# Seven block products for eight in part of a fused retention and two-FFN kernel, with weight steps over pairs of tiles

## The chip, the cores and the metric

One core of a Trainium2 chip runs the whole program. The metric is device time in microseconds, and less is better. A difference of more than 0.3% can be told from no change.

## What is computed

Block retention gives `x` (1536 tokens by 512), and two feed-forward layers follow. Only the first layer's `h` is computed in another way by the change.

```python
h = x @ w_in                                  # 1536x512 @ 512x2048
sp = np.where(h > 20.0, h, np.log1p(np.exp(np.minimum(h, 20.0))))
x = (h * np.tanh(sp)) @ w_out                 # mish; 2048x512
h = x @ w_in                                  # second layer, its own weights
return np.where(h > 0.0, h, np.exp(np.minimum(h, 0.0)) - 1.0) @ w_out
```

The weights are 64-bit floats in memory.

## The kernel before, in words

Every large matrix product is made of 128x512 matmuls on fp32r operands. Each operand is kept as two parts, a high part that ScalarE rounds (Copy to fp32r) and a low part that VectorE subtracts, and one product of two tiles is three matmuls: high by high, high by low, low by high.

After the retention (some 52 us) come two layers. A layer has 4 groups `g` of 4 tiles `i` of d_ff (128 columns each), and the tokens are 3 blocks `t` of 512. A unit is either ("in", s, i), 12 matmuls that make `h` of one tile and one token block (`mm_in`), followed by the activation and the split of `g` into two parts (`split_g`), or ("out", s, d), 12 matmuls over the group's 4 tiles (`mm_out`) whose result `flush` copies or adds to `acc`. The first group makes all 12 "in" units, then "out" of block 0 as one unit of 48 (`all_out`). After that the list `seq` alternates four "in" units of one block with four "out" units of the block before.

The weights come as 64-bit words. `w_load` brings one 128x512 tile (512 KB) into `raw`, which has 4 buffers. `w_steps` makes fp32 of it in eight VectorE instructions and one ScalarE copy, and leaves `w` with its two parts. There are 64 tiles, n = 0 to 63: per layer and group four of `w_in` (side 0) and four of `w_out` (side 1). The tables `FIRST`, `SECOND` and `LATER` say behind which unit each tile's steps are issued. A scheduler then sets the final order on each engine, and each engine runs its own list in order. The names that the engines' lists show, such as `w_1471`, are buffers: the digits tell them apart.

Of the kernel before, what the change touches and what calls it, by code (L numbers as in the profile page):

```python
# [18 lines left out]
def kernel(  # L19
# [37 lines left out]
    order = []  # L57
# [5 lines left out]
    AHEAD = 4  # L63
    wts = {}
    raw = {}

    def w_load(n, part=0, parts=1):
        if n >= NW:
            return
        l, g, side, i = order[n]  # L70
        m = g * G + i
        if part == 0:
            raw[n] = cv.tile([P, KD, P, 2], I32, tag="raw", name="raw", bufs=AHEAD)
        r = raw[n]
# [11 lines left out]
    def w_steps(n, parts=1):  # L86
        if n >= NW:
            return
        l, g, side, i = order[n]
        r = raw[n].rearrange("p k f t -> p (k f) t")  # L90
        tiles = [cv.tile([P, DM], I32, tag=x, name=x) for x in ("m", "b", "u")]
        w = wp.tile([P, 2, DM], F32R, tag=f"w{side}", name=f"w{side}", bufs=(6, 8)[side])
        for y in range(parts):
            cols = slice(y * DM // parts, (y + 1) * DM // parts)
            lw, hw = r[:, cols, 0].bitcast(U32), r[:, cols, 1]
            m, b, u = (x[:, cols] for x in tiles)
            mf, bf, uf = (x.bitcast(F32) for x in (m, b, u))
            yield nc.vector.tensor_scalar(
                out=m, in0=hw, scalar1=1, scalar2=1,
                op0=ALU.logical_shift_left, op1=ALU.logical_shift_right,  # L100
            )
            yield nc.vector.tensor_scalar(out=mf, in0=mf, scalar1=LEAST, scalar2=None, op0=ALU.max)

            yield nc.vector.tensor_scalar(  # L104
                out=b, in0=m, scalar1=3, scalar2=0x3FFFFFF8,
                op0=ALU.logical_shift_left, op1=ALU.bitwise_and,
            )
# [3 lines left out]
            yield nc.vector.tensor_scalar(  # L111
                out=u, in0=b, scalar1=-0x800000, scalar2=None, op0=ALU.bitwise_and
            )

            yield nc.vector.scalar_tensor_tensor(  # L115
                out=uf, in0=lw, scalar=2.0 ** -52, in1=uf, op0=ALU.mult, op1=ALU.mult
            )
            if n >= PG - AHEAD:
                w_load(n + AHEAD)
            yield nc.vector.tensor_tensor(out=mf, in0=bf, in1=uf, op=ALU.add)  # L120
            nc.scalar.activation(out=w[:, 0, cols], in_=mf, func=AF.Copy)  # L121
            yield nc.vector.tensor_tensor(  # L122
                out=w[:, 1, cols], in0=mf, in1=w[:, 0, cols].bitcast(F32), op=ALU.subtract
            )
        del raw[n]
        wts[l, side, g * G + i] = w


    def retention(beside_load, beside_step, at_end):
# [282 lines left out]
    gt, mid, late, acc, entered = {}, {}, {}, [], [0]  # L412

    def open_late():
        def pool(name, **kw):
            return ctx.enter_context(tc.tile_pool(name=name, reuse_waits="tile", **kw))

        late["y"] = pool("yp", bufs=1)
        late["g"] = pool("gp", bufs=12)
        late["psH"] = pool("psL", bufs=3, space=PSUM)  # L420
        late["psY"] = pool("psY", bufs=4, space=PSUM)
        acc.extend(late["y"].tile([P, KD, TB], F32, name=f"acc{t}") for t in range(NTB))

    def mm_in(s, i):
        l, g, t = steps[s]
        w = wts[l, 0, g * G + i]
        h = (late["psH"] if entered[0] % 4 else psH).tile([P, TB], F32, tag="h", name="h")
        entered[0] += 1
        for kk in range(KD):
            wa, wb = (w[:, n, kk * P:(kk + 1) * P] for n in range(2))  # L430
            xa, xb = xh[t][:, kk], xl[t][:, kk]
            for n, (lt, rt) in enumerate(((wa, xa), (wa, xb), (wb, xa))):
                nc.tensor.matmul(  # L433
                    h, lhsT=lt, rhs=rt,
                    start=(kk == 0 and n == 0), stop=(kk == KD - 1 and n == 2),
                )
        return h

    def split_g(s, i):
        g = mid.pop((s, i))  # L440
        gg = late["g"].tile([P, 2, TB], F32R, tag="g", name="g")
        nc.scalar.activation(out=gg[:, 0], in_=g, func=AF.Copy)  # L442
        nc.vector.tensor_tensor(  # L443
            out=gg[:, 1], in0=g, in1=gg[:, 0].bitcast(F32), op=ALU.subtract
        )
        gt[s, i] = gg


    def mish(s, i, h):
        g = tp.tile([P, TB], F32, tag="g32", name="g32", bufs=6)  # L450
        nc.scalar.activation(out=g, in_=h, func=AF.Mish)  # L451
        mid[s, i] = g


    def elu(s, i, h):
        e = tp.tile([P, TB], F32, tag="e", name="e", bufs=3)
        nc.scalar.activation(out=e, in_=h, func=AF.Relu, scale=-1.0)  # L457
        nc.scalar.activation(out=e, in_=e, func=AF.Exp, scale=-1.0)  # L458
        g = tp.tile([P, TB], F32, tag="g32", name="g32", bufs=6)
        nc.vector.scalar_tensor_tensor(  # L460
            out=g, in0=e, scalar=-1.0, in1=h, op0=ALU.add, op1=ALU.max
        )
        mid[s, i] = g

    def mm_out(s, d, cols):
        l, g, t = steps[s]
# [50 lines left out]

    seq = [("in", t, i) for i in range(G) for t in range(NTB)]
    HEAD = len(seq)
    tail = [("out", 0), ("out", 1)]  # L520
    for s in range(NTB, NS):
        tail += [("in", s), ("out", s - 1)]
    tail.append(("out", NS - 1))
    for kind, s in tail:
        seq += [(kind, s, x) for x in range(G if kind == "in" else KD)]

    def unit(u):
        kind, s, x = seq[u]
        if kind == "in":
            (mish, elu)[steps[s][0]](s, x, mm_in(s, x))  # L530
            if late:
                split_g(s, x)
        else:

            if s == 0:
                if x == 0:
                    all_out(s)
                return
            ends = (0, 3 * TB // 4, TB) if u == len(seq) - 1 else (0, TB)
            for c0, c1 in zip(ends, ends[1:]):  # L540
                cols = slice(c0, c1)
                flush(s, x, cols, mm_out(s, x, cols))

    FIRST = (0, 0, 0, 0, 0, 1, 3, 5)
    SECOND = (7, 9, 11, 13, 16, 18, 20, 22)
    LATER = (24, 27, 30, 33, 36, 38, 40, 44)
    EARLY = 1
    BESIDE = 4  # L550
    at = {}
    for n in range(BESIDE, NW):
        g, i = divmod(n, PG)
        u = (FIRST, SECOND)[g][i] if g < 2 else LATER[i] + (g - 2) * 24
        at.setdefault(u, []).append(n)
# [7 lines left out]
    def beside():  # L563
        for n in range(BESIDE):
            yield from w_steps(n, HALVES if n == 0 else 1)
# [5 lines left out]
            pin(w_load(*m, HALVES) if isinstance(m, tuple) else w_load(m))  # L571

    made = []

    def beside_step(n, place, pin):
        for _ in range(STEPS.get((n, place), 0)):
            made.append(pin(next(todo)))

    def weights_at(u):
        for n in at.get(u, ()):  # L580
            for _ in w_steps(n):
                pass

    def first_units():
        with tc.issue_after(made[-2].ins):
# [45 lines left out]
```

## Time and profile before

| | us |
|---|---|
| median of 3 runs | 583.49 (582.27 to 583.72) |
| the profiled execution | 583.47 |
| its span, first to last instruction | 581.3 |
| TensorE busy (matmul) | 574.7 |
| VectorE busy | 433.5 |
| ScalarE busy | 232.0 |

The 2.2 us between span and time lie around the program. Busy time counts a matmul as pipelined, so the chain of waits and the start-to-start times say more than the sum.

### The profile page before, as it was taken

To read this page: it belongs to the slowest core of one execution; us is meant where nothing else is said; L and a number is where in the kernel's file an instruction comes from. 1 tells how busy PE (TensorE), PEld (TensorE's weight loads), DVE (VectorE), ACT (ScalarE), POOL (GpSimd) and SP (SyncE) were. 2 spreads that over 40 slices of the span, in tenths; PEclk is the share of its full clock that TensorE was granted. 3 is DMA by queue.
4 is the path that set the end of the run, shared out by engine and by line. 5 is a ranking of instruction groups with operands and counts; after the bars stand their busy time and mean duration, and the time that the engine had idled before them with its cause. 6 is when DMAs were issued, how large, how long until landed. Compare 5 with 4: busy or idle time off the path is not lost.

```text
span 581.3 us, 8152 instructions
## 1 busy us (share of the span) xinstructions
PE 574.7 (99%) x3234; PEld 481.5 (83%) x3234; DVE 433.5 (75%) x806; ACT 232.0 (40%) x391; POOL 18.8 (3%) x28
## 2 busy tenths in 40 slices
PE   8999999999999999999999999999999999999997
PEld 7998888888888888888888888888888888888886
DVE  7779999999399627993599957995499957944332
ACT  4655553444124214223346446545245225335220
POOL 5330000000000000000000000000000000000000
PEclk9999999999999999999999999999999999999999
DMA  9989324333023201321022221321022300000112
GB/s 181 211 199 248 110 73 146 109 109 118 28 73 118 99 2 36 110 89 57 0 73 72 74 72 37 109 83 63 1 72 73 108 37 1 1 0 1 72 55 91
DMA packets 61045, 46.66 MB, mean 80 GB/s; under 512 B 38864, under 2 KB 55504, under 8 KB 61008
## 3 DMA queue, kind: packets, MB, share of 16 engines
q1 hardware_dynamic: 60864, 46.14, 27.6%
q8 instruction: 25, 0.41, 0.3%
q14 instruction: 12, 0.10, 0.1%
q10 hardware_dynamic: 144, 0.00, 0.0%
HBM read 43.00 MB, written 3.15 MB: 79 GB/s over the span
## 4 chain that ended last, share of the span: by engine, by line
PE 96%; DMA 2%; SPq 1%; issue 0%; DVE 0%
PE h L433 45%; PE y L475 43%; PE o L293 3%; PE y L490 2%; PE sc L279 1%; SPq L157 1%; DMA vn<-in_v_dram 1%; DMA qn<-in_q_dram 1%; PE st L325 1%; PE Tp L235 1%; DVE acc L503 0%
## 5 line engine op out<-in xcount | busy, mean ns | idle before, releaser
L433 PE MATMUL h<-xh,w 128*128 128x512 f32 x768 | 240.4, 389 | 0.0
L433 PEld LDWEIGHTS h<-xh,w 128*128 128x128 f32 x768 | 144.1, 188 | 30.1 <-issue 0.2
L433 PE MATMUL h<-xl,w 128*128 128x512 f32 x384 | 149.4, 389 | 0.0
L475 PE MATMUL y<-w,g 128*128 128x512 f32 (+2 forms) x588 | 133.0, 386 | 0.0
L475 PEld LDWEIGHTS y<-w,g 128*128 128x128 f32 x588 | 109.5, 188 | 22.1
L475 PE MATMUL y<-g,w 128*128 128x512 f32 x528 | 121.6, 389 | 0.0
L475 PEld LDWEIGHTS y<-g,w 128*128 128x128 f32 x528 | 99.1, 188 | 20.6
L503 DVE TENSOR_TENSOR acc<-acc,y 128x512 f32<-128x512 f32 (+1 forms) x73 | 49.5, 678 | 58.3 <-PE y L475 58.2
L443 DVE TENSOR_TENSOR g<-g,g 128x512 fp32r<-128x512 f32 x96 | 66.1, 688 | 28.8 <-ACT g L442 26.4
L433 PEld LDWEIGHTS h<-xl,w 128*128 128x128 f32 x384 | 72.1, 188 | 14.9
L121 ACT ACTIVATE w<-m 128x512 fp32r<-128x512 f32 (+1 forms) x65 | 40.4, 622 | 103.2 <-PE h L433 55.2
L442 ACT ACTIVATE g<-g 128x512 fp32r<-128x512 f32 x96 | 60.4, 629 | 16.4 <-DVE g L460 14.8
L122 DVE TENSOR_TENSOR w<-m,w 128x512 fp32r<-128x512 f32 (+1 forms) x65 | 44.2, 679 | 24.3 <-ACT w L121 23.7
L451 ACT ACTIVATE g<-h 128x512 f32<-128x512 f32 x48 | 28.6, 596 | 69.6 <-PE h L433 69.5
L457 ACT ACTIVATE e<-h 128x512 f32<-128x512 f32 x48 | 28.6, 597 | 59.0 <-PE h L433 58.1
L460 DVE SCALAR_TENSOR_TENSOR g<-e,h 128x512 f32<-128x512 f32 x48 | 32.8, 684 | 17.0 <-ACT e L458 17.0
L115 DVE SCALAR_TENSOR_TENSOR u<-raw,u 128x512 f32<-128x512 uint32 (+1 forms) x65 | 44.1, 678 | 0.2
L120 DVE TENSOR_TENSOR m<-b,u 128x512 f32<-128x512 f32 (+1 forms) x65 | 44.1, 678 | 0.2
L108 DVE SCALAR_TENSOR_TENSOR b<-raw,b 128x512 int32<-128x512 int32 (+1 forms) x65 | 44.0, 678 | 0.1
L458 ACT ACTIVATE e<-e 128x512 f32<-128x512 f32 x48 | 30.2, 630 | 1.1
L111 DVE TENSOR_SCALAR u<-b 128x512 int32<-128x512 int32 (+1 forms) x65 | 27.2, 418 | 0.4
L104 DVE TENSOR_SCALAR b<-m 128x512 int32<-128x512 int32 (+1 forms) x65 | 27.2, 418 | 0.4
(50 smaller groups left out, 307.1 us busy)
## 6 DMA issues: line engine op xcount, KB each, us to landing
raw<-in_moe_w_out_dram SPq DMA_DIRECT2D x32, 512.0 KB, 3.3
raw<-in_moe_w_in_dram SPq DMA_DIRECT2D x31, 512.0 KB, 3.8
vn<-in_v_dram SPq DMA_DIRECT2D x12, 256.0 KB, 5.4
kn<-in_k_dram SPq DMA_DIRECT2D x11, 256.0 KB, 5.2
qn<-in_q_dram SPq DMA_DIRECT2D x11, 256.0 KB, 5.2
out_dram<-acc SPq DMA_DIRECT2D x11, 256.0 KB, 2.0
raw<-in_moe_w_in_dram SPq DMA_DIRECT2D x2, 256.0 KB, 5.5
kn<-in_k_dram SPq DMA_DIRECT2D x2, 128.0 KB, 3.3
```

Of the source, the lines that this page charges most:

```text
L108: yield nc.vector.scalar_tensor_tensor(out=b, in0=hw, scalar=-0x40000000, in1=b, op0=ALU.bitwise_and, op1=ALU.bitwise_or)
L115: yield nc.vector.scalar_tensor_tensor(out=uf, in0=lw, scalar=2.0 ** -52, in1=uf, op0=ALU.mult, op1=ALU.mult)
L120: yield nc.vector.tensor_tensor(out=mf, in0=bf, in1=uf, op=ALU.add)
L121: nc.scalar.activation(out=w[:, 0, cols], in_=mf, func=AF.Copy)
L122: yield nc.vector.tensor_tensor(out=w[:, 1, cols], in0=mf, in1=w[:, 0, cols].bitcast(F32), op=ALU.subtract)
L433: nc.tensor.matmul(h, lhsT=lt, rhs=rt, start=(kk == 0 and n == 0), stop=(kk == KD - 1 and n == 2),)
L442: nc.scalar.activation(out=gg[:, 0], in_=g, func=AF.Copy)
L443: nc.vector.tensor_tensor(out=gg[:, 1], in0=g, in1=gg[:, 0].bitcast(F32), op=ALU.subtract)
L458: nc.scalar.activation(out=e, in_=e, func=AF.Exp, scale=-1.0)
L460: nc.vector.scalar_tensor_tensor(out=g, in0=e, scalar=-1.0, in1=h, op0=ALU.add, op1=ALU.max)
L475: nc.tensor.matmul(y, lhsT=lt, rhs=rt, start=(i == 0 and n == 0), stop=(i == G - 1 and n == 2),)
L503: nc.vector.tensor_tensor(out=dst, in0=dst, in1=y, op=ALU.add)
```

## The change

The diff makes three edits.

**Block products.** For groups 1 to 3 of the first layer, and for token blocks 1 and 2, two tiles of d_ff by two halves of the 512 input rows by the two token blocks are a 2x2 by 2x2 block product. It is computed with seven block products of 6 matmuls each (`block_product`, sums as in Strassen's method in Winograd's form) where eight were. There are two such pairs, z = 0 and 1, in each group. The sums of weight blocks (`block_sums`) are made for every pair, and the sums of token blocks (`token_sums`) once. They lie in new tiles `s`, `t2`, `t3`, `t4`, and one of them in the place of a block of `xh` and `xl`. Products that belong to several results are kept by a ScalarE copy out of their PSUM bank (`keep`), and added by VectorE (`done`). Block 0 keeps its "in" units.

**Weight steps over pairs.** The eight instructions of `w_steps` now handle two tiles, 128x1024, except for tiles 0 to 3. `raw` has two buffers of a pair each, the integer steps write back into `raw`, and the two loads of a pair are issued together when the pair two ahead is done with its buffer. The pairs of `w_out` have two buffers in the first layer.

**Order of units.** All of group 0's "out" units come first. Then each group has three "in" units of block 0, the block products of z = 0, the "out" of block 0 among those of z = 1, and the "out" of blocks 1 and 2. The place of the weight steps is in `PAIRS`.

The core of the diff:

```diff
+        if n % 2 == 0 and part == 0:
+            raw[n // 2] = cv.tile([P, 2, KD, P, 2], I32, tag="raw", name="raw")
...
+        whole = cv.tile([P, 2 * DM], I32, tag="m", name="m")
         for y in range(parts):
...
+            cols = slice(lead + y * count // parts, lead + (y + 1) * count // parts)
+            lw, b, m = r[:, cols, 0].bitcast(U32), r[:, cols, 1], whole[:, cols]
...
             yield nc.vector.scalar_tensor_tensor(
-                out=b, in0=hw, scalar=-0x40000000, in1=b, op0=ALU.bitwise_and, op1=ALU.bitwise_or
+                out=b, in0=b, scalar=-0x40000000, in1=m, op0=ALU.bitwise_and, op1=ALU.bitwise_or
             )
...
+            if both and n >= PG - 4:
+                w_load(n + 4)
+                w_load(n + 5)
+            nc.scalar.activation(out=w0, in_=mf, func=AF.Copy)
+            if both and side == 0 and mixed(l, g):
+                sums[g, i // 2] = block_sums(whole.bitcast(F32))
+            yield nc.vector.tensor_tensor(out=w1, in0=mf, in1=w0.bitcast(F32), op=ALU.subtract)
...
+    def block_sums(w):
+        x = cv.tile([P, 2 * DM], F32, tag="m", name="x")
+        s1, s2, s3, s4 = (x[:, y * 2 * P:(y + 1) * 2 * P] for y in range(4))
+        a11, a12, a21, a22 = (w[:, y * 2 * P:(y + 1) * 2 * P] for y in range(4))
+        plus(s1, a21, a22)
+        minus(s3, a11, a21)
+        minus(s2, s1, a11)
+        minus(s4, a12, s2)
+        t = late["s"].tile([P, 2, 4, 2 * P], F32R, tag="s", name="s")
+        in_two([t[:, n].rearrange("p y c -> p (y c)") for n in range(2)], x)
+        return t
...
+    def block_product(g, z, x):
...
+        bank = {1: 0, 6: 0, 7: 0, 4: 0, 2: 1, 5: 2, 3: 2}[x]
+        fresh = x in (1, 2, 5)
...
+        for kk in range(2):
+            ha, la = (t[:, kk * P:(kk + 1) * P] for t in a)
+            hb, lb = (t[:, kk] for t in b)
+            for n, (lt, rt) in enumerate(((ha, hb), (ha, lb), (la, hb))):
+                nc.tensor.matmul(
+                    ps, lhsT=lt, rhs=rt, start=fresh and kk == 0 and n == 0,
+                    stop=kk == 1 and n == 2, skip_group_check=True,
+                )
...
+        def keep(y):
+            mx[z, "c", y] = tp.tile([P, TB], F32, tag="e", name="c", bufs=ES)
+            nc.scalar.activation(out=mx[z, "c", y], in_=ps, func=AF.Copy)
+
+        def done(y, s, i):
+            c = mx[z, "c", y]
+            nc.vector.tensor_tensor(out=c, in0=c, in1=ps, op=ALU.add)
+            nc.scalar.activation(out=c, in_=c, func=AF.Mish)
...
+    MIX = ((1, 2), (6, 5), (7,), (4, 3))
...
+        seq.extend(("in", s, x) for x in range(3))
+        seq.extend(("mix", (g, 0), x) for x in range(3))
+        seq.append(("in", s, 3))
+        seq.append(("mix", (g, 0), 3))
+        seq.extend(("out", s, d) for d in range(3))
+        seq.extend(("mix", (g, 1), x) for x in range(3))
+        seq.append(("out", s, 3))
+        seq.append(("mix", (g, 1), 3))
...
+    PAIRS = {
+        0: (None, None, 0, 3), 1: (12, 12, 23, 25), 2: (37, 41, 47, 49), 3: (61, 65, 71, 73),
+        4: (82, 84, 88, 91),
+    }
+    TOKENS = 11
```

`in_two` is a ScalarE Copy to fp32r for the high part and a VectorE subtraction for the low part. `token_sums` is ten additions or subtractions of 128x1024 and four `in_two` of 128x1024.

**Where TensorE takes up the outputs of group 1.** Before, the first `w_out` tile of group 1 is `w_1471`, and its first matmuls stand behind the "in" units of two token blocks and behind the outputs of block 2 of group 0:

```order
L433 MATMUL h<-xh_65,w_1442 128x512 x2
L433 MATMUL h<-xl_68,w_1442 128x512
L433 MATMUL h<-xh_65,w_1442 128x512
L475 MATMUL y<-g,w_1471 128x512 x3
L475 MATMUL y<-g,w_1514 128x512 x3
L475 MATMUL y<-g,w_1561 128x512 x3
L475 MATMUL y<-g,w_1612 128x512 x3
```

In the change the first pair of `w_out` tiles of group 1 is `w_1530`. Its matmuls stand among the block products of z = 0 (`mby`) and z = 1 (`mbh`), whose operands are the token sums `t` and the weight sums `s`:

```order
L574 MATMUL mbh<-xh_65,w_1396 128x512
L574 MATMUL mby<-t_1297,s 128x512 x6
L574 MATMUL mby<-t_1298,s 128x512 x6
L615 MATMUL y<-g,w_1530 128x512 x4
L574 MATMUL mby<-t_1299,w_1374 128x512 x6
L574 MATMUL mbh<-xh_66,s 128x512
L574 MATMUL mbh<-xl_69,s 128x512
L574 MATMUL mbh<-xh_66,s 128x512 x2
L574 MATMUL mbh<-xl_69,s 128x512
L574 MATMUL mbh<-xh_66,s 128x512
L615 MATMUL y<-g,w_1530 128x512 x14
```

The outputs of block 2 of group 0 now stand ahead of all "in" units of group 1, so that the outputs of group 1 begin behind the "in" units of only one block and 42 matmuls of block products.

**VectorE ahead of that place.** Before, the low part of `w_1471` is subtracted between the splits of the first "in" units of group 1 (`g_1553` and `g_1586`):

```order
L120 TENSOR_TENSOR m<-b,u 128x512
L108 SCALAR_TENSOR_TENSOR b<-raw,b 128x512
L443 TENSOR_TENSOR g<-g_1553,g 128x512
L111 TENSOR_SCALAR u<-b 128x512
L122 TENSOR_TENSOR w_1471<-m,w_1471 128x512
L115 SCALAR_TENSOR_TENSOR u<-raw,u 128x512
L98 TENSOR_SCALAR m<-raw 128x512
L120 TENSOR_TENSOR m<-b,u 128x512
```

In the change the low part of `w_1530` stands behind the steps of a second pair that was taken up beside it, behind a split of a sum of products (`g<-c`) and behind the addition of products (`c<-c,mby`):

```order
L132 TENSOR_SCALAR m<-raw 128x1024
L129 SCALAR_TENSOR_TENSOR raw<-raw,m 128x1024
L587 TENSOR_TENSOR c<-c,mby 128x512
L136 SCALAR_TENSOR_TENSOR m<-raw,m 128x1024
L161 TENSOR_TENSOR g<-g_1607,g 128x512
L132 TENSOR_SCALAR m<-raw 128x1024
L139 TENSOR_TENSOR m<-raw,m 128x1024
L161 TENSOR_TENSOR g<-c,g 128x512
L136 SCALAR_TENSOR_TENSOR m<-raw,m 128x1024
L146 TENSOR_TENSOR w_1530<-m,w_1530 128x1024
L139 TENSOR_TENSOR m<-raw,m 128x1024
L587 TENSOR_TENSOR c<-c,mby 128x512
```

The subtraction has moved from the beginning of the group's "in" units to their end.

**VectorE at the token sums.** In the change this stands behind the last steps of group 0's weights (`w_1140`). The tile `acc_1082` is the scratch of the token sums, `raw` and `m` belong to the steps of group 1's first pair of `w_in`:

```order
L151 TENSOR_TENSOR acc_1082<-xh_66 128x1024
L151 TENSOR_TENSOR acc_1082<-xl_69 128x1024
L129 SCALAR_TENSOR_TENSOR raw<-raw,m 128x1024
L151 TENSOR_TENSOR acc_1082<-acc_1082 128x1024
L132 TENSOR_SCALAR m<-raw 128x1024
L151 TENSOR_TENSOR acc_1082<-xl_69,xl_68 128x1024
L136 SCALAR_TENSOR_TENSOR m<-raw,m 128x1024
L161 TENSOR_TENSOR t_1298<-acc_1082,t_1298 128x1024
L139 TENSOR_TENSOR m<-raw,m 128x1024
L151 TENSOR_TENSOR acc_1082<-xh_66,xh_65 128x1024
```

No such rows were there before.

**ScalarE at the same place as `w_1530`.** The rounding of its high part stands between two copies of products out of their PSUM bank:

```order
L583 ACTIVATE c<-mby 128x512
L160 ACTIVATE g<-g_1607 128x512
L588 ACTIVATE c<-c 128x512
L160 ACTIVATE g<-c 128x512
L583 ACTIVATE c<-mby 128x512
L143 ACTIVATE w_1530<-m 128x1024
L583 ACTIVATE c<-mby 128x512
L510 ACTIVATE g_1674<-h 128x512
```

Before, nothing but activations, splits and flushes stood around such a copy.

## Rows read from the trace of the kernel before

**Rows 1.** The page's head: busy time of each engine, and VectorE in 40 slices

```profile
span 581.3 us, 8152 instructions
PE 574.7 (99%) x3234; PEld 481.5 (83%) x3234; DVE 433.5 (75%) x806; ACT 232.0 (40%) x391; POOL 18.8 (3%) x28
...
DVE  7779999999399627993599957995499957944332
```

**Rows 2.** The chain that ended last, in order: start us, us, what

```profile
52.19 2.98 PE o L293 x48
55.17 32.89 PE h L433 x144
88.06 10.88 PE y L490 x48
...
103.70 8.16 PE y L475 x36
```

**Rows 3.** Windows of the span: us, busy time by engine, granted clock, DMA

```profile
0.00:52.00 52.00, 48.32 (x870) 45.19 (x870) 39.74 (x64) 28.24 (x47) 18.81 (x28) 1.00 0.97 205
8.00:16.00 8.00, 6.45 (x115) 5.79 (x117) 7.63 (x10) 3.69 (x6) 4.15 (x4) 1.00 1.15 202
52.00:131.00 79.00, 79.00 (x387) 65.41 (x384) 76.21 (x156) 36.30 (x63) 0.00 (x0) 1.00 0.38 120
131.00:229.00 98.00, 98.00 (x434) 81.16 (x433) 68.73 (x131) 30.66 (x51) 0.00 (x0) 1.00 0.20 65
229.00:327.00 98.00, 98.00 (x434) 81.16 (x433) 80.52 (x153) 38.43 (x63) 0.00 (x0) 1.00 0.23 70
```

**Rows 4.** VectorE's groups by form: busy us, mean ns, idle before

```profile
L108 DVE SCALAR_TENSOR_TENSOR b<-raw,b 128x512 int32<-128x512 int32 x63 | 43.2, 686 | 0.1
...
L98 DVE TENSOR_SCALAR m<-raw 128x512 int32<-128x512 int32 x63 | 26.6, 422 | 0.2
L102 DVE TENSOR_SCALAR m<-m 128x512 f32<-128x512 f32 x63 | 26.6, 422 | 0.1
...
L122 DVE TENSOR_TENSOR w<-m,w 128x256 fp32r<-128x256 f32 x2 | 0.8, 416 | 0.0
L102 DVE TENSOR_SCALAR m<-m 128x256 f32<-128x256 f32 x2 | 0.6, 294 | 0.1
```

**Rows 5.** VectorE in order of time: start us, us, what

```profile
52.81 1.22 DVE L286 TENSOR_TENSOR am<-sc,dm 128x1024 f32<-128x1024 f32 x1
53.94 0.28 DVE L111 TENSOR_SCALAR u<-b 128x256 int32<-128x256 int32 x1
...
55.99 0.42 DVE L98 TENSOR_SCALAR m<-raw 128x512 int32<-128x512 int32 x1
56.45 0.43 DVE L102 TENSOR_SCALAR m<-m 128x512 f32<-128x512 f32 x1
...
62.10 0.68 DVE L443 TENSOR_TENSOR g<-g,g 128x512 fp32r<-128x512 f32 x1
62.70 0.42 DVE L98 TENSOR_SCALAR m<-raw 128x512 int32<-128x512 int32 x1
63.04 0.68 DVE L108 SCALAR_TENSOR_TENSOR b<-raw,b 128x512 int32<-128x512 int32 x1
...
70.51 0.42 DVE L98 TENSOR_SCALAR m<-raw 128x512 int32<-128x512 int32 x1
...
114.82 0.69 DVE L122 TENSOR_TENSOR w<-m,w 128x512 fp32r<-128x512 f32 x1
```

**Rows 6.** ScalarE's groups by form

```profile
L241 ACT ACTIVATE T<-Tp 128x1024 f32<-128x1024 f32 x11 | 11.3, 1025 | 5.8 <-PE Tp L235 5.7
```

**Rows 7.** ScalarE in order of time

```profile
111.90 0.60 ACT L501 ACTIVATE acc<-y 128x512 f32<-128x512 f32 x1 [2.12 <-PE y L475]
```

**Rows 8.** DMA issues between 46 and 62 us, median us to landing

```profile
raw<-in_moe_w_in_dram SPq DMA_DIRECT2D x3, 512.0 KB, 6.3
raw<-in_moe_w_out_dram SPq DMA_DIRECT2D x2, 512.0 KB, 3.8
```

More of the change, by code (lines that the diff above doesn't have):

```diff
@@ L62, with mixed @@
     PG = 2 * G
-    AHEAD = 4
     wts = {}
     raw = {}
+    made_w = {}
+    sums = {}
+    late = {}
+    def mixed(l, g):
+        return l == 0 and g > 0
     def w_load(n, part=0, parts=1):
@@ L83, in w_load, with w_tile, w_steps @@
         return nc.sync.dma_start(out=r.rearrange("p k f t -> p (k f t)"), in_=src)
-    def w_steps(n, parts=1):
+    def w_tile(n):
+        l, g, side, i = order[n]
+        if n % 2 == 0:
+            if l == 0:
+                pool, tag, bufs = wp, f"w{side}", 2
+            elif side == 0:
+                pool, tag, bufs = wp, f"w{i // 2}", 2
+            else:
+                pool, tag, bufs = late["w"], "w2", 4
+            made_w[n // 2] = pool.tile([P, 2, 2, DM], F32R, tag=tag, name=tag, bufs=bufs)
+        return made_w[n // 2]
+    def w_steps(n, parts=1, both=False):
         if n >= NW:
@@ L117, in w_steps @@
             )
[L118 to L126, printed above, removed]
+            yield nc.vector.tensor_tensor(out=mf, in0=bf, in1=mf, op=ALU.add)
@@ new lines, in w_steps, with plus @@
+            if both and n >= PG - 4:
[5 more added lines that the diff above has]
+            yield nc.vector.tensor_tensor(out=w1, in0=mf, in1=w0.bitcast(F32), op=ALU.subtract)
+        for j in range(1 + both):
+            wts[l, side, g * G + i + j] = w[:, :, (n + j) % 2]
+    def plus(out, a, b, op=ALU.add):
+        nc.vector.tensor_tensor(
+            out=out.bitcast(F32), in0=a.bitcast(F32), in1=b.bitcast(F32), op=op
+        )
@@ L411 @@
     NS = len(steps)
-    gt, mid, late, acc, entered = {}, {}, {}, [], [0]
+    gt, mid, acc, entered = {}, {}, [], [0]
+    ES = 7
     def open_late():
@@ L437, in mm_in, with g_tile @@
         return h
-    def split_g(s, i):
[L440 to L445, printed above, removed]
+    def g_tile(s, i):
+        if s == 0 and i >= 2:
+            if i == 2:
+                first.append(late["t"].tile([P, 2, 2, TB], F32R, tag="t4", name="gt"))
+            return first[0][:, i - 2]
+        return late["g"].tile([P, 2, TB], F32R, tag="g", name="g")
@@ new lines, in block_product, with of @@
+    def block_product(g, z, x):
+        w = [wts[0, 0, g * G + 2 * z + j] for j in range(2)]
+        sm = sums[g, z]
+        def of(j, h):
+            return [w[j][:, n, h * 2 * P:(h + 1) * 2 * P] for n in range(2)]
+        a = {1: of(0, 0), 2: of(0, 1), 4: of(1, 1)}.get(x)
+        if a is None:
+            y = {5: 0, 6: 1, 7: 2, 3: 3}[x]
+            a = [sm[:, n, y] for n in range(2)]
+        b = mx["b"][x]
+        bank = {1: 0, 6: 0, 7: 0, 4: 0, 2: 1, 5: 2, 3: 2}[x]
+        fresh = x in (1, 2, 5)
+        if fresh:
+            pool, tag = ((late["psY"], "y"), (late["psH"], "h"))[z]
+            mx[z, bank] = pool.tile([P, TB], F32, tag=tag, name="mb" + tag)
+        ps = mx[z, bank]
+        for kk in range(2):
[5 more added lines that the diff above has]
+                    stop=kk == 1 and n == 2, skip_group_check=True,
+                )
+        s1, s2 = g * NTB + 1, g * NTB + 2
+        i1, i2 = 2 * z, 2 * z + 1
+        def keep(y):
[5 more added lines that the diff above has]
+            nc.scalar.activation(out=c, in_=c, func=AF.Mish)
+            mid[s, i] = c
+            split_g(s, i)
+        if x in (1, 6, 7):
+            keep({1: 1, 6: 2, 7: 3}[x])
+        if x == 2:
+            done(1, s1, i1)
+        elif x == 3:
+            done(2, s2, i1)
+        elif x == 4:
+            mish(s1, i2, ps)
+            split_g(s1, i2)
+        if x == 7:
+            ps = mx[z, 2]
+            done(3, s2, i2)
@@ L573 @@
     made = []
+    last_step = {}
     def beside_step(n, place, pin):
@@ L579, in weights_at @@
     def weights_at(u):
+        if u == LAST_MIX:
+            late["mix"].close()
+            late["w"] = ctx.enter_context(tc.tile_pool(name="w2p", reuse_waits="tile", bufs=1))
         for n in at.get(u, ()):
-            for _ in w_steps(n):
+            for last_step[n] in w_steps(n, both=True):
                 pass
+        if u == TOKENS:
+            with tc.issue_after(last_step[PG - 2].ins):
+                token_sums()
     def first_units():
```

116 lines of the change are left out of this document (80 added, 36 removed).

## The prediction

> **What bounds the kernel now.** I read the page's head first: TensorE is busy for 574.7 of 581.3 us [rows 1]. Busy time flatters matmuls, so I went to the chain of waits. From 55 us it is one run of TensorE's own matmuls, and 48 of them always take 10.88 us, 0.2267 us each [rows 2]. The windows confirm it: TensorE is idle for 3.7 us in the first 52 us, and for nothing in the stretches shown between 52 and 327 us [rows 3]. So a matmul removed is worth 0.2267 us, as long as its operands are there in time. What could make them late is VectorE, which runs the weight steps. It is busy for 76.2 of 79.0 us between 52 and 131 us, 96%, and for 70% and 82% of the next two stretches [rows 3]. It is nevertheless early there: the low part of `w_1471` is made at 114.8 us [rows 5], and its first matmul stands 240 matmuls behind the start of `all_out`, at 88.06 + 240 x 0.2267 = 142.5 us [rows 2]. That lead of 27 us is what the change can spend.
>
> **What it removes.** Per pair z, eight block products of 6 matmuls become seven. With two pairs in three groups that is 6 x 6 = 36 matmuls of 1152, of the same shape as those left: 36 x 0.2267 = **8.16 us**. By this alone the profiled execution's 583.47 us become 575.3 (span 573.1). Its time agrees with the median, 583.49, so no correction is needed.
>
> **What it adds to VectorE.** What counts is the time from one start to the next, which is shorter than the duration. A two-input instruction of 512 takes 0.60 us (62.10 to 62.70), a one-input one 0.34 (62.70 to 63.04), and 0.12 more when the next needs its result (55.99 to 56.45 is 0.46); a two-input one of 1024 takes 1.13 (52.81 to 53.94) [rows 5]. A one-input one of 256 is 0.128 us shorter than one of 512 [rows 4], so at 1024 I take 0.34 + 2 x 0.128 = 0.60. A two-input one of 256 is 0.27 shorter than one of 512 (416 against 686 ns) [rows 4], 0.33.
>
> A pair of tiles thus costs 4 x 0.60 + 4 x 1.13 = 6.9 us, against 2 x (4 x 0.34 + 4 x 0.60) = 7.5 for two single tiles. Over 30 pairs this gives back 18 us. The token sums cost 14 x 1.13 = 15.8 us once; the weight sums 4 x 0.33 + 1.13 = 2.45 us for each of six pairs, 14.7; the additions of products 18 x 0.60 = 10.8. In all VectorE has some 23 us more than its 433.5 [rows 1]. Averaged over the span that is nothing, but all the token sums and two of the weight sums fall into the stretch that is at 96%.
>
> **Where it ends on the path.** I followed VectorE's order from the first instruction that differs in size, the one on `raw` of tiles 4 and 5, at 70.51 us [rows 5]; up to there the work is the same. From it to the low part of `w_1530` there are 38 two-input instructions of 1024, 24 one-input ones of 1024, 14 two-input ones of 512 and 8 of 256, and 18 times one needs the result of the one just before: 42.9 + 14.4 + 8.4 + 2.6 + 2.2 = 70.5 us, so 141.0.
>
> To this come waits for ScalarE, which is not busy but runs in order behind copies that TensorE paces. A flush starts 0.04 us after its last matmul (111.86, the end of the chain's piece at 103.70, then 111.90) [rows 2, 7]. The rounding of the token sum that replaces `xh_66` stands behind the flush of block 1's third output, whose matmuls end at 88.06 + 84 x 0.2267 = 107.1. With 0.6 for the flush [rows 7] and 1.03 for a 1024 copy [rows 6] it is ready at 108.8, and VectorE would be there at 108.0: 0.8 us. The splits of group 1's first two "in" units end at 124.7 and 127.5 by the same working (matmuls end at 123.4 and 126.1), VectorE is there at 123.8 and 127.2: 0.9 and 0.3. Together 2.0, and the low part of `w_1530` is done at 141.0 + 2.0 + 0.1 = 143.1 us.
>
> TensorE wants it for its third `w_1530` matmul. Ahead of that, from the start of `all_out`, stand 48 matmuls of `all_out`, 96 of blocks 1 and 2, 48 "in" matmuls, 42 of block products and 2 of `w_1530`: 236 x 0.2267 = 53.5, so 141.6 us. TensorE waits for **1.5 us**. Behind that matmul in its order stand the block products of both pairs; nothing overtakes.
>
> The places ahead have more room. The low part of `w_1140` is done at 92.6 and wanted at 95.3. The first product with token and weight sums is wanted at 128.9, and its sums end by 114. Behind the wait VectorE gains on TensorE: a group has four pairs (29 us with the dependences), two weight sums (5), 6 additions, 12 splits and 12 flushes (18), 52 us in 276 matmuls or 62.6 us. In groups 2 and 3 the `w_out` pair must wait for its buffer until block 2's outputs are done; 46 matmuls (10.4 us) later it is wanted, and VectorE needs some 7 us from there. In layer 2 a group has 51 us of VectorE work in 65.3. These I cost at nothing; without that room each us late is a us lost.
>
> **Loads.** They are as many and as large, but two are issued at once, when a pair's buffer is done. For tiles 6 and 7 VectorE asks 5.0 us after that, for 8 and 9 5.3 us. Single loads land after 3.8 us, three issued close together after 6.3 [rows 8]. I take something between for two and no wait; by 6.3 it is 1.3 + 1.0 = 2.3 us more, which is kept for the range.
>
> **The write into `raw`.** One of the eight steps now writes every second word. No row has such a write. Reading so costs nothing: 422 ns strided and dense [rows 4]. The lower bound is therefore nothing; the upper is half speed, 1.07 us per 1024. Up to `w_1530` that is 3 single tiles and 6 pairs, 8.0 us, of which the 2.0 of waits for ScalarE would be taken up: a wait of 7.5 us. I take nothing, by the reading rows, the nearest ones. The Trainium skill (SBUF — State Buffer, Door 1: The DMA port swizzle) says that fp32 can be strided up to four elements without cost, since accesses that share a 16-byte line run at full bandwidth; by it the sum stays 576.8.
>
> **The sum.** 583.47 - 8.16 + 1.5 = **576.8 us**.
>
> **Rivals.**
>
> *No wait at all* (575.3). If ScalarE's copies come a little earlier, or VectorE's 1024 forms cost less than taken, 1.5 us of 72 are gone. Nothing in the rows excludes this, 2% on the sum suffices.
>
> *The strided write costs half speed, or loads are late* (579 to 583). 575.3 + 1.5 + 2.3 = 579.1 with late loads, 575.3 + 7.5 = 582.8 with the slow write. Against the write speak the strided reads.
>
> *Handing over PSUM banks* (slower, up to 588). Three of seven products share one bank with copies between: product, ScalarE copy of 0.6 us, next product, and there are 18 such copies. The order puts 4 or more other matmuls (0.9 us) behind most, but ScalarE runs in order, and the copy can stand behind one that waits for VectorE, as that of `w_1530` does. If every copy lay open, 18 x 0.6 = 10.8 us, 576.8 + 10.8 = 587.6. The gain of 6.7 is gone from 0.37 us per copy on. ScalarE's 40% [rows 1] speaks against it.
>
> *The clock falls.* TensorE was idle for 1.55 of 8 us at 8 to 16 us, and its granted clock stayed at 1.00 (2.4 GHz) [rows 3]. If the wait at 141 us let it fall to 1.2 GHz for the next 48 matmuls, they would take 10.9 us more, 587.7. The Trainium skill (TensorE: Matmul & The Clock Gate, Part 1: The HAM clock gate) says that idling throttles the array to half rate until it has been busy again; by that rule 587.7 would be the time, but the idle stretches of this trace show no fall.
>
> *The change does not do what it says.* The built order has 864 + 252 = 1116 matmuls for `h` in both layers, against 1152, and as many output matmuls as before, so this one gets no chance.
>
> **Chances.** A wait of about 0.7 to 4 us, 576 to 579.3: 0.55. None, below 576: 0.22. Late loads or part of the other costs, up to 581.7: 0.10. The slow write, or half of the copies open: 0.06. Copies open, above 585.2: 0.05. The clock, also above: 0.02. A change of 0.3% (1.75 us) is about what can be told from none, so faster means below 581.7: 0.87; same 0.06; slower 0.07. The range that leaves out no more than 2 in 10 reaches from 574.8 (matmul pace a little better) to 581.5.
>
> **What would show it.** Right: 36 fewer first-layer matmuls at 0.2267 us; one wait of TensorE for VectorE (`w`, low part) near 141 us of 1 to 3 us and no other above 0.5; VectorE at nearly 100% from 70 to 143 us; strided steps of 1024 at 1.22 us. Wrong: waits of the block products (`mby`, `mbh`) for ScalarE in each pair, a step on `raw` above 2 us, VectorE idle behind a load, or a clock below 1.00.

## The result and the profile after

The changed kernel takes **576.58 us** (median of 4 runs, 576.26 to 577.16) against 583.09 for the one before: a ratio of 0.989, 95% interval 0.9873 to 0.9907, faster by 6.5 us. The forecast was 576.8. The number was right; the place and the kind of the loss in it were not, as the views show.

The page's head, as in [rows 1]:

```profile
span 573.7 us, 7842 instructions
PE 567.1 (99%) x3198; PEld 474.7 (83%) x3198; DVE 455.3 (79%) x628; ACT 246.0 (43%) x389; POOL 18.8 (3%) x28
```

36 matmuls are gone from TensorE (3234 to 3198) and 21.8 us have come to VectorE. The chain of waits begins as in [rows 2], half a microsecond earlier, and has one piece that isn't TensorE's own (start us, us, what):

```profile
54.67 32.86 PE h L487 x144
...
137.86 1.37 PE mby L574 x6
139.23 0.02 issue
139.25 0.61 ACT c L583
139.86 0.04 issue
139.90 1.65 PE mby L574 x6
141.56 0.91 PE y L615 x4
142.47 1.43 PE mby L574 x6
143.90 1.38 PE mbh L574 x6
...
270.85 1.44 PE mby L574 x6
...
548.38 22.45 PE y L615 x108
```

The retention stage, up to the first `h`, took 54.3 to 56.4 us in the profiles of this study, whatever the kernel. So from here on I also compare **from h**: from the start of the first `h` to the end of the last `y`. Before, the first `h` begins at 55.17 [rows 2], and the last run of `y` is

```profile
555.90 22.45 PE y L475 x108
```

so 555.90 + 22.45 - 55.17 = 523.18 us. After, 548.38 + 22.45 - 54.67 = 516.16. The difference is 7.02 of the 8.16 us forecast for 36 matmuls, so 1.14 us were lost. The rows from 137.86 to 143.90 us hold 1.06 of it: 0.67 between two block products (0.02 + 0.61 + 0.04) and 0.39 in the matmuls around it, where runs of six took 1.65, 1.43, 1.38 and 1.37 in place of 1.36. The other 0.08 is in the run of six at 270.85, which took 1.44.

TensorE's waits after 52 us are this one alone (engine, line, waited for: us in total, times, longest):

```profile
PE mby L574 <- ACT c L583: 0.7, 1, 0.7
```

L583 is the copy that keeps a product: product 6 of the first pair ends, ScalarE copies its PSUM bank (the place where TensorE adds up a product's matmuls), and product 7 may only then go on in that bank. In the code product 5 stands between the two; the built order has it earlier. Nothing stood ahead of the copy on ScalarE, which had been idle for 2.06 us until product 6 ended:

```profile
139.25 0.60 ACT L583 ACTIVATE c<-mby 128x512 f32<-128x512 f32 x1 [2.06 <-PE mby L574]
```

So here the loss comes from TensorE's order alone, two products of one bank with nothing between. There was no wait for `w_1530`. VectorE around it, and TensorE's first two runs that read `w_1530` (start us, us, what):

```profile
140.99 1.22 DVE L146 TENSOR_TENSOR w<-m,w 128x1024 fp32r<-128x1024 f32 x1
142.13 1.22 DVE L139 TENSOR_TENSOR m<-raw,m 128x1024 f32<-128x1024 f32 x1
...
144.73 0.70 DVE L119 TENSOR_SCALAR m<-raw 128x1024 int32<-128x1024 int32 x1 [0.79 <-DMA raw<-in_moe_w_in_dram]
...
141.39 1.07 PE L615 MATMUL y<-g,w 128*128 128x512 f32 x4
...
145.11 3.33 PE L615 MATMUL y<-g,w 128*128 128x512 f32 x14
```

The low part is the L146 row, done at 142.21. But the four `y` matmuls from 141.39 on all read the high part: in the built order they are high x high and high x low of two outputs, and the row agrees, since all four had started by 142.1, before the low part was done. The first that reads the low part is in the next run of `y`, of 14, which starts at 145.11. So there were at least 2.9 us of room where the prediction had a wait.

The windows, as in [rows 3] (us, busy time of PE, PEld, DVE, ACT, POOL, granted clock, DMA):

```profile
70.00:143.00 73.00, 72.31 (x319) 59.47 (x318) 70.40 (x86) 33.93 (x50) 0.00 (x0) 1.00 0.24 82
...
200.00:320.00 120.00, 120.00 (x531) 99.23 (x530) 107.19 (x148) 51.26 (x80) 0.00 (x0) 1.00 0.21 71
320.00:570.00 250.00, 250.00 (x1111) 207.54 (x1109) 165.37 (x221) 100.86 (x162) 0.00 (x0) 1.00 0.15 54
```

VectorE is at 96% from 70 to 143 us, TensorE idle for 0.69 there and never after, the clock at 1.00. VectorE's groups, as in [rows 4]; L129 is the write of every second word into `raw`:

```profile
L129 DVE SCALAR_TENSOR_TENSOR raw<-raw,m 128x1024 int32<-128x1024 int32 x30 | 36.5, 1222 | 0.2
L136 DVE SCALAR_TENSOR_TENSOR m<-raw,m 128x1024 f32<-128x1024 uint32 x30 | 36.3, 1220 | 0.2
...
L125 DVE TENSOR_SCALAR m<-m 128x1024 int32<-128x1024 int32 x30 | 20.6, 688 | 0.0
...
L151 DVE TENSOR_TENSOR x<-m 128x256 f32<-128x256 f32 x12 | 4.5, 420 | 0.1
```

### The profile page after: what moved, and what is told of

It reads as the page before. It is cut to its first block, busy times and chain, and to the rows that moved or that the text cites. A ratio compares the mean times of both kernels' runs of the same rounds, so it can differ in the third digit from the quotient of the medians.

```text
span 573.7 us, 7842 instructions
## 1 busy us (share of the span) xinstructions
PE 567.1 (99%) x3198; PEld 474.7 (83%) x3198; DVE 455.3 (79%) x628; ACT 246.0 (43%) x389; POOL 18.8 (3%) x28
## 4 chain that ended last, share of the span: by engine, by line
PE 97%; SPq 1%; DMA 1%; issue 0%; ACT 0%; DVE 0%
PE y L615 44%; PE h L487 34%; PE mby L574 5%; PE mbh L574 5%; PE o L341 4%; PE y L630 2%; PE sc L327 2%; SPq L205 1%; DMA qn<-in_q_dram 1%; PE Tp L283 1%; PE st L373 1%; ACT c L583 0%; DVE acc L643 0%
## 5 line engine op out<-in xcount | busy, mean ns | idle before, releaser
L487 PE MATMUL h<-xh,w 128*128 128x512 f32 x576 | 181.7, 389 | 0.0
L487 PEld LDWEIGHTS h<-xh,w 128*128 128x128 f32 x576 | 108.1, 188 | 22.6 <-issue 0.2
L487 PE MATMUL h<-xl,w 128*128 128x512 f32 x288 | 112.0, 389 | 0.0
L516 DVE SCALAR_TENSOR_TENSOR e<-e,h 128x512 f32<-128x512 f32 x48 | 32.7, 685 | 25.9 <-ACT e L515 25.9
L146 DVE TENSOR_TENSOR w<-m,w 128x1024 fp32r<-128x1024 f32 (+2 forms) x35 | 39.5, 1130 | 8.5 <-ACT w L143 8.5
L143 ACT ACTIVATE w<-m 128x1024 fp32r<-128x1024 f32 (+2 forms) x35 | 34.4, 983 | 24.6 <-PE y L615 16.6
L161 DVE TENSOR_TENSOR g<-e,g 128x512 fp32r<-128x512 f32 x48 | 33.0, 689 | 12.2 <-ACT g L160 12.0
L129 DVE SCALAR_TENSOR_TENSOR raw<-raw,m 128x1024 int32<-128x1024 int32 (+2 forms) x35 | 39.4, 1130 | 0.2
L136 DVE SCALAR_TENSOR_TENSOR m<-raw,m 128x1024 f32<-128x1024 uint32 (+2 forms) x35 | 39.2, 1129 | 0.2
L139 DVE TENSOR_TENSOR m<-raw,m 128x1024 f32<-128x1024 f32 (+2 forms) x35 | 39.1, 1128 | 0.2
(105 smaller groups left out, 576.6 us busy)
```

Source lines behind the costliest of these rows:

```text
L129: yield nc.vector.scalar_tensor_tensor(out=b, in0=b, scalar=-0x40000000, in1=m, op0=ALU.bitwise_and, op1=ALU.bitwise_or)
L136: yield nc.vector.scalar_tensor_tensor(out=mf, in0=lw, scalar=2.0 ** -52, in1=mf, op0=ALU.mult, op1=ALU.mult)
L139: yield nc.vector.tensor_tensor(out=mf, in0=bf, in1=mf, op=ALU.add)
L143: nc.scalar.activation(out=w0, in_=mf, func=AF.Copy)
L146: yield nc.vector.tensor_tensor(out=w1, in0=mf, in1=w0.bitcast(F32), op=ALU.subtract)
L161: nc.vector.tensor_tensor(out=t[1], in0=x, in1=t[0].bitcast(F32), op=ALU.subtract)
```

## The experiments

Two theories at the start. **A**: matmuls are the time, and all that is lost is the hand-over of one PSUM bank. **B**, the prediction's step: TensorE waits for VectorE's low part of `w_1530`, so each us of VectorE ahead of it costs one.

**The changed kernel again**, beside later variants:

> The changed kernel itself, beside the variants on the same chip: 576.6 us within 0.6, one wait of TensorE for ScalarE's copy of 0.7 us, 516.2 us from the first matmul of h to the last of y.

576.10 us (ratio 0.9881, 0.9861 to 0.9902), the same wait of 0.7, 516.20 from h.

**The block products undone, pairs kept.**

```
 def mixed(l, g):
-    return l == 0 and g > 0
+    return False
...
-for y in MIX[x]:
-    block_product(*s, y)
+step, i = g * NTB + 1 + x % 2, 2 * z + x // 2
+mish(step, i, mm_in(step, i))
+split_g(step, i)
```

> The block products are undone (the h of the second and third thirds of the tokens is made by 12 matmuls a matrix again, 36 matmuls more; no sums of tokens or weights, no additions), the weight steps over pairs of tiles, their loads and the order of units stay. If the products' matmuls alone are the gain: 576.6 + 8.16 = 584.7 us, less the 1.1 us that the changed kernel lost at the hand-over between block products, so 583.6 us and no wait of TensorE above 0.2 us after 52 us. Rival (the weight steps over pairs bring or take a part of their own): 582 us or less where the pairs alone gain 1 us or more, 585 us or more where they lose.

583.07 us, ratio 1.0004 (0.9991 to 1.0016). From h: 555.27 + 22.45 - 54.56 = 523.16, where before had 523.18, and no wait of TensorE. So the weight steps over pairs, their loads and the new order of units, which all stay here, together bring nothing and take nothing, and the whole gain is the products'. (The median is 0.5 us below the 583.6 expected; the medians of the kernel before differ by as much from one measurement to the next, 583.0 to 583.5.)

**Weight steps in halves, products kept.**

```
-for last_step[n] in w_steps(n, both=True):
+for last_step[n] in w_steps(n, 2, both=True):
```

> The steps on a pair of weight tiles run as two halves of 512 columns each in place of one of 1024; products, loads and order of units stay. By the rows VectorE pays 0.60 us for each half of a two-input step against 1.13 for the whole and 0.34 against 0.60 for a one-input step, some 0.6 us a pair or 18 us in all. Theory B: the low part of w_1530 comes 3 us or more later and TensorE waits for it, 579 to 580 us. Theory A: VectorE has room for that everywhere: its busy time rises, TensorE's waits do not, 576.6 us, at most 577.5.

576.65 us (0.9886, 0.9872 to 0.9901). VectorE is busy for 467.7 us, 12.4 more, and makes the two halves of the low part of `w_1530` like this:

```profile
141.38 0.70 DVE L146 TENSOR_TENSOR w<-m,w 128x512 fp32r<-128x512 f32 x1
...
143.79 0.70 DVE L146 TENSOR_TENSOR w<-m,w 128x512 fp32r<-128x512 f32 x1
```

The first half is done at 142.08, about when the whole was in the changed kernel; the second at 144.49, counted from h 2.6 us later. TensorE waits for neither: its waits after 52 us are two, of 1.1 us in all, both for the copy of a product. Theory B doesn't hold. From h, though, this kernel takes 549.20 + 22.45 - 54.38 = 517.27, 1.1 more than the changed kernel, which the median doesn't show. Its second wait, of 0.46 us, ends at 271.47, in the layer's last group, between products 7 and 4, which share a bank as well. There the built order has one other matmul between the two; the changed kernel has four at the same place, and no wait. With none between, products 6 and 7 wait for 0.69 us.

**The low part made three times, and seven times.**

```
+for _ in range(2 if n == 12 else 0):    # 6 in the other kernel
+    nc.vector.tensor_tensor(out=w1, in0=mf, in1=w0.bitcast(F32), op=ALU.subtract)
 yield nc.vector.tensor_tensor(out=w1, in0=mf, in1=w0.bitcast(F32), op=ALU.subtract)
```

> The subtraction that makes the low part of the pair w_1530 is done three times in place of once, 2.3 us of VectorE ahead of it. Theory B (TensorE waits for it already): 576.6 + 2.3 = 578.9 us. Theory A (2.9 us of room in the order of the changed kernel): the low part comes some 2.3 us later or more, where the extra steps are spread among others as the six were; up to 149 us nothing waits for it, time 576.6 us within 0.6. A wait of TensorE for the low part, if it comes after 150 us.

> VectorE's subtraction that makes the low part of the pair w_1530 is done seven times in place of once, six times 1.13 us = 6.8 us more ahead of the step that the prediction held to be the one TensorE waits for; the result doesn't change. Theory B: each of them costs its time, 576.6 + 6.8 = 583.4 us, less at most 1 us. Theory A (the first matmul that wants the low part stands later than the prediction read, with 2.9 us of room in the order of the changed kernel and more where the order moves high parts ahead): 576.6 us, at most 577.5, and no wait of TensorE for VectorE above 1 us.

Three times: 577.33 us (0.9895, 0.9875 to 0.9915), TensorE's only wait after 52 us is again the 0.7 us copy. By B 578.9, which lies outside its runs (575.89 to 577.55); 0.7 us above A's 576.6, which these runs don't tell from it (A had said within 0.6). From h it takes 548.32 + 22.45 - 54.34 = 516.43, 0.3 more than the changed kernel. Its two low parts on VectorE behind the extra steps (L148), that of the second pair and that of `w_1530`:

```profile
145.68 2.36 DVE L148 TENSOR_TENSOR w<-m,w 128x1024 fp32r<-128x1024 f32 x2 [0.26 <-ACT w L143]
```

The one of `w_1530` is the second, as the weight load that waits for it below shows, done at 148.04, counted from h 6.2 us later than in the changed kernel. By the prediction's step TensorE would have waited for some 6 us. The built order has moved: two `y` matmuls stand at 144.80 and 24 at 148.10, where the low part is just in time: a weight load waits for it for 0.4 us, no matmul does. So each of these kernels also tests another order of TensorE.

Seven times: **587.76** us (1.0074, 1.006 to 1.0088), slower than both theories said. The six extra steps (L147) were not run together, but spread among other work, and the true low part came last:

```profile
142.27 1.23 DVE L147 TENSOR_TENSOR w<-m,w 128x1024 fp32r<-128x1024 f32 x1
...
157.85 1.23 DVE L147 TENSOR_TENSOR w<-m,w 128x1024 fp32r<-128x1024 f32 x1
...
161.32 1.23 DVE L148 TENSOR_TENSOR w<-m,w 128x1024 fp32r<-128x1024 f32 x1
```

So this run moved the start of the low part, counted from h, by 19.1 us (140.99 - 54.67 to 161.32 - 55.92), not by 6.8. TensorE's waits between 120 and 180 us:

```profile
PE y L617 <- DVE w L148: 4.7, 1, 4.7
PE mbh L576 <- DVE c L589: 1.7, 1, 1.7
PE mbh L576 <- ACT c L585: 1.0, 2, 0.8
PE mby L576 <- ACT c L585: 0.7, 1, 0.7
```

and the windows at the longest of them:

```profile
158.00:162.50 4.50, 0.00 (x0) 0.00 (x0) 4.50 (x6) 0.63 (x1) 0.00 (x0) 0.90 0.00 0
162.50:166.00 3.50, 3.40 (x8) 2.73 (x9) 3.40 (x5) 0.30 (x1) 0.00 (x0) 0.50 0.00 0
166.00:170.00 4.00, 4.00 (x14) 3.12 (x14) 4.00 (x8) 1.82 (x2) 0.00 (x0) 0.70 0.74 262
```

From h it takes 527.97, 11.8 more than the changed kernel: 7.4 of waits (8.1 in these rows against 0.7), and 3.0 since the granted clock stood at 0.50 (1.2 GHz) behind the idle stretch, so that the next 42 `y` matmuls took 12.53 us in place of 9.52; 1.4 are not put to a row. So the cover has an end, and A's limit of 577.5 was wrong for this kernel. TensorE itself waits for the low part only here, with that part 19 us late.

**The order of the products, three times.** In all three the changed kernel's wait should go, or move.

```
 ins = nc.tensor.matmul(ps, ...)
+if (g, z) == (1, 0) and x in (6, 5, 7):
+    tc.keep_in_program_order(ins)
```

> Only products 6, 5 and 7 are held in the order of the program: product 5 now stands between 6 and 7, and product 4 follows 7 in the same bank with nothing between. Theory A (the wait belongs to any two products that follow each other directly in one bank): the wait of about 0.7 us moves to between products 7 and 4, time unchanged at 576.6 us within 0.4. If the wait were of product 6 alone, it would be gone and the time some 575.5 us. Theory B (low part of w_1530): no wait of this kind matters, 576.6 us.

575.87 us (0.9872, 0.9857 to 0.9888), 516.08 from h; the wait of 0.67 now lies behind products 6, 5 and 7, in front of 4:

```profile
136.48 4.09 PE mby L574 x18
...
140.59 0.61 ACT c L585
...
141.25 1.65 PE mby L574 x6
```

The time lies between the two that were expected (576.6 and 575.5); from h it is that of the changed kernel, and the wait has moved as A says.

With product 4 and the last `h` of the first third held too (`x in (6, 5, 7, 4)`, and the same line in `mm_in`):

> Block products 6, 5 and 7 of the first pair of group 1, the last matrix of h of the first third and product 4 are held in the order of the program on TensorE, so that six or more other matmuls stand between two products that follow each other in PSUM bank 0. Nothing else is changed. Theory A (the only loss left is the hand-over of the bank between products 6 and 7: 0.67 us of waiting and about 0.47 us of restart): 1.1 us less than the changed kernel, some 575.5 us, and no wait of TensorE for ScalarE's copy of product 6 or 7 above 0.1 us. Theory B (the step of the prediction: TensorE waits near 141 us for the low part of w_1530): the order of the products doesn't matter, 576.6 us as before the edit.

576.64 us (0.9888, 0.9872 to 0.9904), 516.58 from h. Not A's 575.5: the wait went to product 6, which had been drawn forward, and grew to 1.2 us. ScalarE's rows say why:

```profile
132.85 0.60 ACT L512 ACTIVATE g<-h 128x512 f32<-128x512 f32 x1 [3.22 <-PE h L487]
133.35 0.59 ACT L587 ACTIVATE c<-mby 128x512 f32<-128x512 f32 x1
```

The copy of product 1 stands behind a Mish that waits for an `h` of TensorE's; product 6 starts at 133.99, 0.05 us after the copy. Third, with the products of the second pair set between by hand:

```
+behind = {(1, 0, 7): (1, 5), (1, 1, 6): (0, 7), (1, 0, 4): (1, 6)}.get((*s, y))
 with ExitStack() as es:
+    if behind:
+        es.enter_context(tc.issue_after(mx[behind[0], "last", behind[1]].ins))
     block_product(*s, y)
```

> In the second group TensorE's order is set by hand: product 7 of the first pair stands behind product 5 of the second, product 6 of the second behind it, and product 4 of the first behind that, so that six matmuls or more stand between any two products that follow each other in a bank, and product 6 keeps its place behind the products of the second pair. Theory A (the loss of 1.1 us is this one hand-over): no wait of TensorE for ScalarE above 0.1 us after 52 us, 515.0 us from the first matmul of h to the last of y in place of 516.2, and a time of 575.4 us, 1.1 less than the changed kernel. Theory B (low part of w_1530): the time stays, as the low part comes no earlier; here it is wanted at about 143.7 us, so if it is the limit, TensorE waits for it.

576.79 us (0.9882, 0.9861 to 0.9903), 516.56 from h. A's number was missed again: the wait, 1.2 us, is now that of the second pair's product 5 for a free bank. ScalarE has the Mish that frees it behind the copy of product 6:

```profile
140.06 0.60 ACT L583 ACTIVATE c<-mby 128x512 f32<-128x512 f32 x1 [2.06 <-PE mby L574]
140.55 0.59 ACT L510 ACTIVATE g<-h 128x512 f32<-128x512 f32 x1
```

So A had the resource right, a PSUM bank, and for two products side by side the cause too, but a wait for a bank is left with other matmuls between. What makes the bank late in these last two kernels is ScalarE's order: the instruction that frees it stands behind one that waits for TensorE itself (theory C, tried last).

**Block products in the second layer too**, to see whether the count of matmuls goes on to be the time as VectorE fills up:

```
 def mixed(l, g):
-    return l == 0 and g > 0
+    return g > 0
...
+if u == TOKENS[1]:
+    token_sums()
```

with weight buffers as in the first layer and ELU in `done`.

> Second layer's h of the second and third thirds of the tokens by the seven block products too, from its second group on: 36 matmuls fewer, 8.16 us by 0.2267 us each. VectorE gets the sums of tokens once more (15.8 us, in the second layer's first group), and for each of three groups 5 us of sums of weights and 3.6 us of additions: 42 us on top of 165 busy in 250. Theory A (TensorE's matmuls are the time as long as VectorE has room, and it has here): 568.4 us, up to 570 with a few hand-overs of 0.7 us. Theory B (VectorE sets the end where it is near full, and each us there costs one): the first group of the second layer has 43 us of work by its mean share, 59 with the sums, in 65 us; where the steps come late as in the first layer 572 us or more.

574.69 us (0.9849, 0.9831 to 0.9866); by A 568.4. From h 515.02: of 8.16 us only 1.1 came. TensorE's waits between 440 and 572 us:

```profile
PE y L613 <- ACT g L155: 2.0, 1, 2.0
PE y L613 <- DVE c L582: 1.6, 2, 0.8
PE mby L568 <- ACT c L578: 1.4, 2, 0.7
PE y L613 <- DVE acc L641: 0.3, 1, 0.3
```

None is for a weight tile, though VectorE is now busy for 86%. By their rows the 1.6, the 1.4 and the 0.3 us look like hand-overs of banks, some now through ELU's longer chain; the 2.0 us is a wait for `g` itself, in the tail of the last group, behind which nothing else is left to run. Two changes there:

```
+if gq == 2 * NG - 1:
+    ...
+    seq.extend([(*z0, 3), (*z1, 0), (*z1, 1), o[0], (*z1, 2), o[1], (*z1, 3), o[2], o[3]])
```

> The second layer by block products too, as before, but in its last group the outputs of the first third, 48 matmuls in all, are put between and behind the block products of the second pair of tiles, where TensorE waited 4.5 and 5.3 us for a chain of ScalarE and VectorE. Theory A (the second layer's products lose at waits of which those of the last group have nothing else to run, not at VectorE's load): 8.16 us less than the changed kernel, plus two hand-overs of about 1.1 us and at most 2 us at the end, 570.5 to 572.5 us. Theory B (VectorE's load in the second layer): 574 to 575 us as without the new order, and the waits move elsewhere.

572.09 us (0.9807, 0.979 to 0.9823), 512.53 from h: the waits of 2.0 and 0.3 are gone, the other two rows stand. (The 4.5 and 5.3 us of the expectation were lengths of chain pieces, with other matmuls running beside them; the waits of the last group were some 1.5 and 2.3.) And without products in the last group:

```
-return g > 0
+return g > 0 and (l, g) != (1, NG - 1)
```

> The second layer by block products in its second and third groups alone, the last group by eight products as in the changed kernel: 24 matmuls fewer than it, 5.44 us, two hand-overs of about 1.1 us more, 573.3 us by theory A; by theory B (VectorE's load, which the last group shares least) no better than 574.7 us, as with all three groups.

573.21 us (0.9825, 0.9808 to 0.9842). Here the last group's `h` of the last third is computed from a tile in which a token sum stands by then, so that part of the output means nothing; the instructions are of the usual number and shape. A's 573.3 was met; but from h it takes 545.88 + 22.45 - 54.65 = 513.68, so only 2.5 of the 5.44 us came, and its waits in the second layer are 1.9 us, of which 0.8 and 0.4 are for VectorE's additions of products and 0.7 for a copy.

**ScalarE's order as well.** The kernel with the new last group, in the second group TensorE's order as in the third try (with product 5 of the second pair held behind product 6 of the first, and the fourth "in" unit of block 0 put ahead of the block products in `seq`), and:

```
+if (l, g) in HAND and (z, x) == (0, 6):
+    es.enter_context(tc.issue_after(mx[s1 - 1, 3].ins))
 nc.scalar.activation(out=mx[z, "c", y], in_=ps, func=AF.Copy)
```

so that the Mish of the last `h` comes ahead of the copy of product 6, and in the built order ahead of that of product 1.

> The kernel with block products in both layers and the new order of its last group, and in the second group of the first layer both orders by hand: on TensorE product 6 of the first pair, product 5 of the second, product 7 of the first, product 6 of the second, product 4 of the first, and on ScalarE the Mish that frees the bank of the last h of the first third ahead of the copy of product 1. Theory C (TensorE's loss in the second group is the hand-over of a PSUM bank through ScalarE, which moves with the order as long as a bank's copy stands behind another one that is itself waiting; it goes when six matmuls stand between two products of a bank and no copy that a free bank hangs on stands behind one that waits): no wait of TensorE between 130 and 165 us, 1.1 to 1.2 us less than without, 571.0 us. Rival (some wait for a bank is left in any order, as VectorE and ScalarE are full there): a wait of 0.7 to 1.2 us at a new place, 572.1 us.

**571.20 us** (570.92 to 571.43), ratio 0.9799, 0.9785 to 0.9813: the fastest kernel of the study. Its chain at the place, and the window:

```profile
137.74 1.36 PE mby L569 x6
139.10 1.36 PE mbh L569 x6
140.46 1.36 PE mby L569 x6
141.82 1.36 PE mbh L569 x6
143.18 0.91 PE y L617 x4
```

```profile
137.00:146.00 9.00, 9.00 (x42) 7.44 (x41) 9.00 (x12) 7.00 (x13) 0.00 (x0) 1.00 0.51 152
```

No wait, and every product takes 1.36. From h 511.44, 1.09 less than the same kernel without these orders, which is the loss that the changed kernel has (1.14). So with both orders the wait goes, as theory C had it, and the rival's wait at a new place did not come. Which of the edits did it is not separated, since ScalarE's order was not changed alone. That the rest of the second layer's loss is of the same kind is read from the waits and was not tried.

## Why the prediction was right, and where it was wrong

- **The pace and the count** were right: 36 x 0.2267 = 8.16 us, all but 1.14 of it seen from h. With the products undone the time from h is that of before to 0.02 us.
- **VectorE's sum** was right: 21.8 us more against "some 23"; 1.22 us for two-input steps of 1024, 0.69 for one-input ones, 0.42 for those of 256, and starts 1.14 apart. Its waits for ScalarE were 0.7, 1.0 and 0.2 (forecast 0.8, 0.9, 0.3). The low part of `w_1530` was forecast for 143.1; with `h` half a us earlier that is 142.6, and it came at 142.21, though VectorE had also waited 0.54 us for a load at 86.55, where the forecast had no wait.
- **The step that failed** is "TensorE wants it for its third `w_1530` matmul". The order row says only that four matmuls read `w_1530`; I took the third for the one on the low part, as in the code's loop, but the scheduler had put the high-part matmuls of two outputs first. Wanted at 145.1 or later, not 141.6: room of 2.9 us or more in place of a wait of 1.5. With the subtraction made three times it came 6.2 us later, in another order, and no matmul waited for it.
- **The loss came from a rival**, handing over PSUM banks, which had a chance of 0.05 and 10.8 us if all 18 copies lay open. One of 18 did, for 0.67 us and 0.39 in the matmuls around it. The reason that I gave ("the copy can stand behind one that waits") is not what happened here, since nothing stood ahead of that copy; in two of the later orders a bank was late for such a reason, behind an instruction that waited for TensorE. (Four of the seven products share one bank, 1, 6, 7 and 4, where I had three; the copies between are three.) The order of TensorE shown with the change has the place: product 6 (`t_1297`, six matmuls) directly ahead of product 7 (`t_1298`). I priced the copies by most places, which have others between, and let this one pass. A wait of 1.5 us that wasn't there and a loss of 1.1 that was not forecast gave the right total, which was luck.
- **The write into `raw`** costs nothing: 1222 ns against 1220 for the dense step. The Trainium skill (SBUF — State Buffer, Door 1: The DMA port swizzle) says that fp32 can be strided up to four elements without cost; these rows agree for a step of two.
- **Loads**: two at once land after 4.1 and 4.9 us in the median (before 3.3 and 3.8). VectorE waited for them 3.4 us in all, 0.79 at most, while TensorE had other work.
- **The clock** stayed at 1.00, and the wait of 0.7 us is too little to say more. With the subtraction made seven times it fell to 0.50 behind 4.7 us of idling, ahead of which stood shorter waits (0.8, 0.2 and 1.7 us in the 8 us before), and that cost 3.0 us. The price that I gave, 10.9 us, was over three times that. The Trainium skill (TensorE: Matmul & The Clock Gate, Part 1: The HAM clock gate) says that idling throttles the array to half rate; this trace agrees.
- **Room in later groups** was there, if less than said: VectorE was busy for 107.2 of the 120 us from 200 to 320, mostly groups 2 and 3, which is 56 in 62.6 where I had 52.

## What to carry to other kernels

A due time needs the operand of the very matmul: of a product made of high and low parts, look which matmul in the built order is the first to read the low one. Where a bank goes from TensorE to another engine and back, count the matmuls between (with none TensorE waited for 0.69 us, with one for 0.46, with four not at all), then look what stands ahead of the copy in its engine's queue and what that waits for; here a new order on TensorE alone moved the wait three times, and orders on TensorE and ScalarE together ended it. A trial that delays one instruction is built anew, so read in its own trace how far that instruction moved and whether the order around it is still the same. Fewer matmuls are time only as long as there is other work for the hand-overs to lie beside, which is what the last group lacks.

## What the runs showed of the hardware

Behind a wait of 0.67 us the next six matmuls took 1.65 us in place of 1.36, at a granted clock of 1.00, so with what the runs of six around it lost, the wait cost 1.06 us. Behind one of 4.7 us the clock stood at 0.50, and a run of 42 matmuls lost 3.0 us. A step of 1024 that writes every second word took 1222 ns, a dense one 1220. VectorE ran 12.4 us more, in halves, with no difference in the median; from h that kernel took 1.1 us more, part of it in a second hand-over of a bank.
